# A routed attention and expert kernel: the bias of each exponential made on ScalarE instead of VectorE

## The chip, the cores and the metric

The kernel runs on one core of a Trainium2 chip. The metric is device time in microseconds (us) of one execution, as the median of several runs. A core has TensorE (PE in the rows, matrix products), VectorE (DVE), ScalarE (ACT), GpSimd (POOL) and SyncE (SP, which issues DMAs here). Each engine works through its own instructions in program order and waits on semaphores for the others.

## What is computed

Four batches of 12,288 queries attend to 768 pooled keys each (the keys are also the values), and every resulting row goes through one of eight experts, chosen by the largest of eight logits.

```python
kv_pool = kv.reshape(B, H // r, r, W // r, r, C).mean(axis=(2, 4))
k = v = kv_pool.reshape(B, -1, C) @ w_sr
s = scale * (q @ k.transpose(0, 2, 1))
s = s - s.max(-1, keepdims=True)
a = np.exp(s)
a /= a.sum(-1, keepdims=True) + 1e-09
x = (a @ v).reshape(B * S, D)
# per expert e, for the rows whose largest logit of x @ w_gate is e:
out[mask] = gate_w[mask, None] * eom[mask, e, None] * (np.maximum(x[mask] @ w1[e], 0.0) @ w2[e])
```

The part in question is `exp(s - s.max())`: for each row of scores the largest one is found, and the exponential is taken of the scaled scores less the scaled maximum.

## The kernel before

The 49,152 tokens are worked on in 96 groups of 512; a group is four blocks of 128 tokens, and four groups make a chunk, which is the unit of the routing (`routing`, 25 of them, since the last chunk is cut in two). The program's order is written out by hand: `for i in range(NG + OL)` goes over the groups, and eight steps `s` within each group emit the instructions of several groups at different stages. No scheduler moves anything afterwards.

In a step, in the order of the letters of `ORD` ("shxryfue"):

- **s**, `qk`, on even steps: TensorE makes the scores `S` of one block (128 tokens by 768 keys, in two PSUM banks, six products, L533 to L537; `S` has two buffers). VectorE takes the negated maximum of each row from PSUM into `nm[:, 0:1]` (L539) and, in an operation on one element per partition (L540), multiplies it by the row's factor `es` (a column of the tile `qm`) and adds the constant `PSH * log 2`: this is the bias, `nm[:, 1:2]`.
- **h**, `moe_h`: TensorE makes one of eight 128-row parts of the hidden layer, `H` (L864 to L866), ScalarE writes its rectified high half `HH` (L869) and VectorE the low half `HL` (L870). When `HL` is done the PSUM buffer of `H` is free. There are three such buffers (`psH`), shared with `U`, the sum over the values, and with the logits.
- **x**, `qk_exp`: ScalarE takes the exponential of the block, with `nm[:, 1:2]` as bias and `es` as scale, and sums the rows (L554). It waits for VectorE (the bias) and for GpSimd (the buffer of `pr`). In every second block `scale()` follows: VectorE's L899, which waits for the exponential.
- **r**, `qk_round`, a step later: ScalarE rounds `pr` to 16 bit (L567), GpSimd makes the remainder.
- **u** and **y**: TensorE's products with the values (L591, into `U`), and the second expert product (L879 to L881, into `Y`), which uses `HH` and `HL` of an earlier step.

`routing` adds some twenty small VectorE operations per chunk between these (L665 to L769), a piece a step. `es` and `nm` are columns of 128 partitions, read as one value per partition.

Of the kernel before, what the change touches and what calls it, by code (L numbers as in the profile page):

```python
# [20 lines left out]
F32 = mybir.dt.float32  # L21
# [4 lines left out]
AF = mybir.ActivationFunctionType  # L26
ALU = mybir.AluOpType
# [5 lines left out]
P = 128  # L33
# [13 lines left out]
PSH = 11  # L47
EPS = 1e-9
BIG = float(1 << 22)
LAG = 2  # L50
# [51 lines left out]
def body(ctx, tc, q, kv, w_sr, w_gate, w_og, w1, w2, out, cfg=Cfg):  # L102
    nc = tc.nc
    pe, act, dve, pool, sp = nc.tensor, nc.scalar, nc.vector, nc.gpsimd, nc.sync
# [22 lines left out]
    cst = ctx.enter_context(tc.tile_pool(name="cst", bufs=1))  # L127
# [45 lines left out]
    for n in sorted(set(n for _, n in UN)):  # L173
        runs[n] = cst.tile([P, E * n * GB], F32, name=f"run{n}")
        dve.memset(runs[n], 1.0)
        dve.memset(runs[n].rearrange("p (e b) -> p e b", e=E)[:, :, 0:1], 0.0)
    c13 = cst.tile([P, CG], F32, name="c13")
    dve.memset(c13, 2.0 ** -13)

# [334 lines left out]
    def qk(i, j):  # L514

        K2 = KVT[i // GPB][0]
        KH, KL = K2[:, 0, :], K2[:, 1, :]
        c, g = divmod(i, CG)
        es = QM[c][:, 2, g:g + 1]
        if j == 0:  # L520
            PTt[i] = wk.tile([P, 2 * NKB, GT], F16, tag="PT", bufs=2, name=f"PT{i}")
            if unit[i][1] == 0:
                SUMS[unit[i][0]] = rt.tile([P, CB], F32, tag="SUM", bufs=4, name=f"SUM{i}")
        S = psA.tile([P, 2, 512], F32, tag="A", name=f"S{i}_{j}")
        hk = [x for x in hooks if x[0] <= now[0]]
        if hk and (j in cfg.HJ or i <= OL):
            hooks.remove(hk[0])
            hk[0][1](S)
        m = i - OL - 1
        scale = moe_turn(m, j - 2, S) if j >= 2 and m >= 0 else None  # L530
        qh, ql = QS[i][:, j, :], QS[i][:, GB + j, :]
        for h in range(2):
            pe.matmul(S[:, h, 0:384], qh, KH[:, ts(h, 384)], start=True, stop=False)  # L533
        for h in range(2):
            pe.matmul(S[:, h, 0:384], qh, KL[:, ts(h, 384)], start=False, stop=False)  # L535
        for h in range(2):
            pe.matmul(S[:, h, 0:384], ql, KH[:, ts(h, 384)], start=False, stop=True)  # L537
        nm = wk.tile([P, 2], F32, tag="nm", bufs=4, name=f"nm{i}_{j}")
        dve.tensor_reduce(out=nm[:, 0:1], in_=S[:, :, 0:384], op=ALU.max, axis=AX.XY, negate=True)  # L539
        dve.tensor_scalar(nm[:, 1:2], nm[:, 0:1], es, PSH * math.log(2.0), op0=ALU.mult, op1=ALU.add)  # L540
        QX[(i, j)] = (S, nm, es, scale)
        if scale and j == GB - 1:
            OST.pop(m)
# [4 lines left out]
    def qk_exp(i, j):  # L548

        S, nm, es, scale = QX.pop((i, j))  # L550
        c, g = unit[i]
        pr = wk.tile([P, NK], F32, tag="pr", bufs=cfg.PRB, name=f"pr{i}_{j}")
        bl = g * GB + j
        act.activation(pr.rearrange("p (a k) -> p a k", a=2), S[:, :, 0:384], AF.Exp,  # L554
                       bias=nm[:, 1:2], scale=es, accum_out=SUMS[c][:, bl:bl + 1])
        PR[(i, j)] = pr
        if scale:
            scale()
# [329 lines left out]
    def moe_turn(i, h, S):  # L888

        ys = OST[i]  # L890
        c, g = unit[i]
        if h == 0:
            OT[i] = wk.tile([P, GB, C], F32, tag="o", name=f"o{i}")
        o = OT[i]
        for j in range(2):
            pe.transpose(S[:, j, 384:512], ys[:, ts(2 * h + j, P)], ident)

        def scale():
            dve.tensor_tensor(o[:, ts(h, 2), :], S[:, :, 384:512],  # L899
                              MSC[c][:, g * GB + 2 * h:g * GB + 2 * h + 2].unsqueeze(2).to_broadcast([P, 2, C]),  # L900
                              op=ALU.mult)
        return scale
# [159 lines left out]
    with tc.manual_schedule(engines={pool.engine, sp.engine, pe.engine, act.engine, dve.engine}):  # L1062
# [82 lines left out]
        for i in range(NG + OL):  # L1145
# [5 lines left out]
            for s in range(8):  # L1151
# [11 lines left out]
                for o in cfg.ORD if mi >= 0 else cfg.ORDA:  # L1163
# [4 lines left out]
                    if o == "s" and att and s % 2 == 0:  # L1168
                        qk(i, s // 2)
                        while late:  # L1170
                            qk_round(*late.pop(0))
                    if o == "x" and att and s % 2 == 0:
                        qk_exp(i, s // 2)
# [86 lines left out]
        while events:  # L1260
            i, s = divmod(min(events), 8)
# [7 lines left out]
def kernel_body(tc, q, kv, w_sr, w_gate, w_og, w1, w2, out, cfg=Cfg):  # L1269
    with ExitStack() as ctx:  # L1270
        body(ctx, tc, q, kv, w_sr, w_gate, w_og, w1, w2,
             out.rearrange("(b n) c -> b n c", b=cfg.NB), cfg)
# [28 lines left out]
```

## Time and profile before

| | us |
|---|---|
| median of three runs (lowest, highest) | 1921.08 (1918.65, 1921.35) |
| the profiled execution, its own time | 1917.69 |
| its span, first to last instruction | 1916.0 |
| TensorE busy in it | 1862.5 (97%) |
| VectorE busy | 1460.6 (76%) |
| ScalarE busy | 1317.8 (69%) |
| GpSimd busy | 1251.3 (65%) |

The granted clock of TensorE is 0.995 of full speed over the span. A busy TensorE is modelled from overlapping products, so what counts for it is the time in which it stood still and who ended that.

### The profile page before, as it was taken

Reading aid. Unit: us, or ns where it says so; the run is one execution under the profiler, and the core shown is the slowest. Engines: PE = TensorE matmul, PEld = TensorE weight load, DVE = VectorE, ACT = ScalarE, POOL = GpSimd, SP = SyncE. Lnnn points to the kernel's source line nnn. Section 1 sums busy time; section 2 is a strip of 40 time slices with the busy share of each in tenths; the row PEclk is TensorE's granted clock in tenths of the full one; section 3 lists DMA queues with packets and bytes.
Section 4 is the critical chain, followed back from the end, with each engine's and each line's share of the span. In section 5 each row is a group of like instructions: output and inputs, shape, how many; then the busy total and the mean of one; then the engine's idle time right before and its main releaser. Section 6 shows DMA issues by size and latency. Waiting matters only on the chain. (4 is left out here: it accounts for less than half of the span.)

```text
span 1916.0 us, 31565 instructions
## 1 busy us (share of the span) xinstructions
PE 1862.5 (97%) x10225; PEld 951.3 (50%) x10225; DVE 1460.6 (76%) x2984; ACT 1317.8 (69%) x2391; POOL 1251.3 (65%) x1426
## 2 busy tenths in 40 slices
PE   6899999999999999999999999999999999999978
PEld 5444455554545555545545555544455455554534
DVE  6776877778878778778787777787787877776754
ACT  3777767677776776676777767766777767676733
POOL 2548677676586777774767867856657557567561
PEclk9999999999999999999999999999999999999999
DMA  8888889888888988887979888877978788877632
GB/s 236 161 161 164 179 167 174 166 161 179 178 164 179 176 159 180 167 165 154 194 149 189 176 178 176 174 152 149 187 146 167 152 160 154 156 153 147 133 73 71
DMA packets 884021, 311.67 MB, mean 163 GB/s; under 512 B 827584, under 2 KB 833857, under 8 KB 883856
## 3 DMA queue, kind: packets, MB, share of 16 engines
q1 hardware_dynamic: 870944, 309.18, 79.8%
q0 software_dynamic: 12480, 0.40, 0.6%
q8 instruction: 81, 1.33, 0.3%
q14 instruction: 84, 0.69, 0.1%
q10 hardware_dynamic: 432, 0.07, 0.0%
HBM read 56.83 MB, written 51.25 MB: 56 GB/s over the span
## 5 line engine op out<-in xcount | busy, mean ns | idle before, releaser
L120 POOL TENSOR_TENSOR ph<-pr,ph 128x384 f16<-128x384 f32 (+1 forms) x760 | 711.6, 936 | 493.1 <-issue 417.5
L870 DVE SCALAR_TENSOR_TENSOR HL<-H,HH 128x512 f16<-128x512 f32 x768 | 526.9, 687 | 166.3 <-ACT HH L869 135.1
L869 ACT ACTIVATE HH<-H 128x512 f16<-128x512 f32 x768 | 456.0, 594 | 234.6 <-PE H L866 197.9
L554 ACT ACTIVATE pr<-S,nm,qm 128x768 f32<-128x768 f32 x384 | 380.6, 991 | 249.3 <-DVE nm L540 219.1
L779 POOL DMA_INDIRECT scr<-rw,idx x384 | 386.2, 1006 | 98.2 <-issue 81.2
L539 DVE TENSOR_REDUCE nm<-S 128x1 f32<-128x768 f32 x384 | 363.2, 946 | 74.3 <-PE S L537 50.1
L591 PE MATMUL U<-PT,V 128*128 128x512 f16 (+1 forms) x1746 | 406.2, 378 | 8.3 <-DVE HL L870 5.1
L567 ACT ACTIVATE ph<-pr 128x768 f16<-128x768 f32 x380 | 320.3, 843 | 2.5 <-DMA PT<-ph 2.0
L864 PE MATMUL H<-U,w 128*128 128x512 f16 x768 | 291.5, 380 | 7.8 <-DVE HL L870 4.4
L879 PE MATMUL Y<-HH,w 128*128 128x512 f16 x768 | 291.3, 379 | 1.8 <-ACT HH L869 1.0
L881 PE MATMUL Y<-HL,w 128*128 128x512 f16 x768 | 291.0, 379 | 0.9 <-DVE HL L870 0.6
L866 PE MATMUL H<-U,w 128*128 128x512 f16 x768 | 291.5, 380 | 0.0
L865 PE MATMUL H<-U,w 128*128 128x512 f16 x768 | 291.5, 380 | 0.0
L880 PE MATMUL Y<-HH,w 128*128 128x512 f16 x768 | 291.1, 379 | 0.0
L591 PEld LDWEIGHTS <-V 128*128 128x128 f16 x1746 | 171.3, 98 | 214.6 <-issue 10.9
L533 PE MATMUL S<-K,qT 128*128 128x384 f16 x768 | 188.1, 326 | 5.8 <-ACT pr L554 3.5
L537 PE MATMUL S<-K,qT 128*128 128x384 f16 x768 | 188.0, 327 | 1.3 <-DVE qT L504 1.0
L535 PE MATMUL S<-K,qT 128*128 128x384 f16 x768 | 188.0, 326 | 0.5 <-DVE K L394 0.5
L899 DVE TENSOR_TENSOR o<-S,msw 128x256 f32<-128x256 f32 x176 | 74.7, 425 | 98.3 <-ACT pr L554 91.3
L120 POOL TENSOR_TENSOR kvs<-kvs 128x256 f32<-128x256 f32 (+2 forms) x148 | 108.1, 731 | 20.9 <-DMA kvs<-in_kv_dram 9.9
L880 PEld LDWEIGHTS <-w 128*128 128x128 f16 x768 | 75.2, 98 | 91.0 <-issue 3.7
L866 PEld LDWEIGHTS <-w 128*128 128x128 f16 x768 | 75.2, 98 | 91.0 <-issue 0.6
(209 smaller groups left out, 1815.4 us busy)
## 6 DMA issues: line engine op xcount, KB each, us to landing
kvs<-in_kv_dram SPq DMA_DIRECT2D x96, 256.0 KB
q<-in_q_dram SPq DMA_DIRECT2D x96, 256.0 KB
urows<-uT SPq DMA_DIRECT2D x96, 256.0 KB
out_dram<-o SPq DMA_DIRECT2D x96, 256.0 KB
PT<-ph SPq DMA_TRANSPOSE x384
scr<-rw,idx POOLq DMA_INDIRECT x384
wr<-in_moe_w_dram SPq DMA_DIRECT2D x8, 512.0 KB
tw<-in_moe_w_dram SPq DMA_DIRECT2D x4, 512.0 KB
```

Of the source, the lines that this page charges most:

```text
L120: ins = pool.tensor_tensor(*a, **k)
L539: dve.tensor_reduce(out=nm[:, 0:1], in_=S[:, :, 0:384], op=ALU.max, axis=AX.XY, negate=True)
L554: act.activation(pr.rearrange("p (a k) -> p a k", a=2), S[:, :, 0:384], AF.Exp, bias=nm[:, 1:2], scale=es, accum_out=SUMS[c][:, bl:bl + 1])
L567: act.activation(ph[:, 0, :], pr, AF.Copy)
L591: pe.matmul(PVP[i][:, cols], ops[n][0], ops[n][1][:, cols], start=(n == 0), stop=(n == len(ops) - 1))
L779: ins = pool.indirect_dma_start(out=scr, out_offset=bass.IndirectOffsetOnAxis(ap=idx[:, bl:bl + 1], axis=0), in_=rw[:, bl, :], in_offset=None,
L864: pe.matmul(H, w1h[:, ts(f, P)], UH, start=True, stop=False)
L865: pe.matmul(H, w1h[:, ts(f, P)], UL, start=False, stop=False)
L866: pe.matmul(H, w1l[:, ts(f, P)], UH, start=False, stop=True)
L869: act.activation(HH, H, AF.Relu)
L870: dve.scalar_tensor_tensor(HL, H, 0.0, HH, op0=ALU.max, op1=ALU.subtract)
L880: pe.matmul(Y, w2l[:, ts(f, P)], HH, start=False, stop=False)
```

## The change

From the fourth group on (`i > LAG`, 93 of 96 groups, 372 of 384 blocks) VectorE no longer makes the bias. ScalarE makes it in front of each exponential, with an `Identity` activation on one element per partition that reads the maximum, a column `shift` holding the constant, and `es`.

```diff
+    shift = cst.tile([P, 1], F32, name="shift")
+    dve.memset(shift, PSH * math.log(2.0))
...
         dve.tensor_reduce(out=nm[:, 0:1], in_=S[:, :, 0:384], op=ALU.max, axis=AX.XY, negate=True)
-        dve.tensor_scalar(nm[:, 1:2], nm[:, 0:1], es, PSH * math.log(2.0), op0=ALU.mult, op1=ALU.add)
+        if i <= LAG:
+            dve.tensor_scalar(nm[:, 1:2], nm[:, 0:1], es, PSH * math.log(2.0), op0=ALU.mult, op1=ALU.add)
...
         bl = g * GB + j
+        if i > LAG:
+            act.activation(nm[:, 1:2], nm[:, 0:1], AF.Identity, bias=shift, scale=es)
         act.activation(pr.rearrange("p (a k) -> p a k", a=2), S[:, :, 0:384], AF.Exp,
                        bias=nm[:, 1:2], scale=es, accum_out=SUMS[c][:, bl:bl + 1])
```

On ScalarE, the first two blocks of group 66 stand like this before (`pr` is the exponential, `ph` its rounding, `HH` the hidden layer's high half, `z` a step of the routing; the numbers behind names are buffers):

```order
L869 ACTIVATE HH_7_16038<-H_7_16034 128x512
L554 ACTIVATE pr_0_16042,SUM_15527<-S_0_16024,nm_0_16031,qm_14338 128x768
L869 ACTIVATE HH_0_16062<-H_0_16058 128x512
L567 ACTIVATE ph_0_16066<-pr_0_16042 128x768
L735 ACTIVATE z_16021<-z_16021 128x16
L869 ACTIVATE HH_1_16091<-H_1_16087 128x512
L554 ACTIVATE pr_1_16095,SUM_15527<-S_1_16075,nm_1_16084,qm_14338 128x768
L884 ACTIVATE ys_16105<-Y_15917 128x512
```

and like this in the changed program:

```order
L874 ACTIVATE HH_7_16039<-H_7_16035 128x512
L558 ACTIVATE nm_0_16033<-nm_0_16033,shift,qm_14340 128x1
L559 ACTIVATE pr_0_16043,SUM_15529<-S_0_16026,nm_0_16033,qm_14340 128x768
L874 ACTIVATE HH_0_16064<-H_0_16060 128x512
L572 ACTIVATE ph_0_16068<-pr_0_16043 128x768
L740 ACTIVATE z_16023<-z_16023 128x16
L874 ACTIVATE HH_1_16092<-H_1_16088 128x512
L558 ACTIVATE nm_1_16086<-nm_1_16086,shift,qm_14340 128x1
L559 ACTIVATE pr_1_16096,SUM_15529<-S_1_16077,nm_1_16086,qm_14340 128x768
L889 ACTIVATE ys_16107<-Y_15919 128x512
```

One operation (L558) stands in front of each exponential (now L559); it waits for VectorE's maximum, and the exponential now waits for ScalarE's own L558 and for GpSimd. Nothing else moved on this engine, and the program holds one load of activation tables as before.

On VectorE, the same two blocks before (`nm` the maximum and the bias, `HL` the hidden layer's low half, `st` a step of the routing):

```order
L539 TENSOR_REDUCE nm_0_16031<-S_0_16024 128x1
L540 TENSOR_SCALAR nm_0_16031<-nm_0_16031,qm_14338 128x1
L870 SCALAR_TENSOR_TENSOR HL_7_16039<-H_7_16034,HH_7_16038 128x512
L460 TENSOR_REDUCE qm_15309<-q_15778 128x1
L466 SCALAR_TENSOR_TENSOR qm_15309<-qm_15309,c_123 128x4
L467 RECIPROCAL qm_15309<-qm_15309 128x4
L733 TENSOR_TENSOR z_16021<-z_16021,rinv_15890 128x16
L870 SCALAR_TENSOR_TENSOR HL_0_16063<-H_0_16058,HH_0_16062 128x512
L539 TENSOR_REDUCE nm_1_16084<-S_1_16075 128x1
L540 TENSOR_SCALAR nm_1_16084<-nm_1_16084,qm_14338 128x1
L870 SCALAR_TENSOR_TENSOR HL_1_16092<-H_1_16087,HH_1_16091 128x512
L711 SCALAR_TENSOR_TENSOR st_15999<-S_1_16075,ebase 128x8
```

and in the changed program:

```order
L541 TENSOR_REDUCE nm_0_16033<-S_0_16026 128x1
L875 SCALAR_TENSOR_TENSOR HL_7_16040<-H_7_16035,HH_7_16039 128x512
L462 TENSOR_REDUCE qm_15311<-q_15780 128x1
L468 SCALAR_TENSOR_TENSOR qm_15311<-qm_15311,c_125 128x4
L469 RECIPROCAL qm_15311<-qm_15311 128x4
L738 TENSOR_TENSOR z_16023<-z_16023,rinv_15892 128x16
L875 SCALAR_TENSOR_TENSOR HL_0_16065<-H_0_16060,HH_0_16064 128x512
L541 TENSOR_REDUCE nm_1_16086<-S_1_16077 128x1
L875 SCALAR_TENSOR_TENSOR HL_1_16093<-H_1_16088,HH_1_16092 128x512
L716 SCALAR_TENSOR_TENSOR st_16001<-S_1_16077,ebase 128x8
```

The one-element operation behind each maximum is gone, and `HL` follows the maximum directly. TensorE, GpSimd and the DMA queues have the same instructions in the same order.

## Rows read from the trace of the kernel before

**Rows 1.** The page: span, and TensorE's busy time

```profile
span 1916.0 us, 31565 instructions
...
PE 1862.5 (97%) x10225; PEld 951.3 (50%) x10225; DVE 1460.6 (76%) x2984; ACT 1317.8 (69%) x2391; POOL 1251.3 (65%) x1426
```

**Rows 2.** Busy time by stretch: the long middle, and one stretch of 80 us

```profile
80.00:1760.00 1680.00, 1666.79 (x9146) 843.42 (x9144) 1312.24 (x2608) 1201.13 (x2175) 1147.43 (x1307) 1.00 0.84 166
...
1440.00:1520.00 80.00, 80.00 (x439) 40.36 (x438) 61.32 (x122) 58.48 (x104) 52.06 (x58) 1.00 0.80 160
```

**Rows 3.** Waits: who for whom, us in total, times, longest

```profile
PE U L591 <- DVE HL L870: 5.1, 7, 1.8
PE H L864 <- DVE HL L870: 4.4, 8, 1.1
...
PE H L864 <- DVE U L596: 2.8, 5, 1.0
...
DVE o L899 <- ACT pr L554: 91.3, 163, 1.6
```

**Rows 4.** Timeline of TensorE, two stalls: start, us, what, idle time before it

```profile
1269.69 0.38 PE L864 MATMUL H<-U,w 128*128 128x512 f16 x1 [0.64 <-DVE HL L870]
...
1270.76 0.38 PE L879 MATMUL Y<-HH,w 128*128 128x512 f16 x1 [0.26 <-ACT ys L884]
```

**Rows 5.** Timeline of VectorE ahead of these two stalls

```profile
1261.15 0.42 DVE L899 TENSOR_TENSOR o<-S,msw 128x256 f32<-128x256 f32 x1 [0.61 <-ACT pr L554]
...
1264.34 0.95 DVE L539 TENSOR_REDUCE nm<-S 128x1 f32<-128x768 f32 x1
1265.33 0.21 DVE L540 TENSOR_SCALAR nm<-nm,qm 128x1 f32<-128x1 f32 x1
1265.46 0.68 DVE L870 SCALAR_TENSOR_TENSOR HL<-H,HH 128x512 f16<-128x512 f32 x1
...
1267.24 0.69 DVE L870 SCALAR_TENSOR_TENSOR HL<-H,HH 128x512 f16<-128x512 f32 x1
1267.85 0.95 DVE L539 TENSOR_REDUCE nm<-S 128x1 f32<-128x768 f32 x1
1268.83 0.21 DVE L540 TENSOR_SCALAR nm<-nm,qm 128x1 f32<-128x1 f32 x1
1268.96 0.68 DVE L870 SCALAR_TENSOR_TENSOR HL<-H,HH 128x512 f16<-128x512 f32 x1
1270.25 0.17 DVE L711 SCALAR_TENSOR_TENSOR st<-S,ebase 128x8 f32<-128x8 f32 x1 [0.61 <-ACT pr L554]
```

**Rows 6.** Timeline of ScalarE ahead of the same two stalls

```profile
1260.04 0.99 ACT L554 ACTIVATE pr<-S,nm,qm 128x768 f32<-128x768 f32 x1 [1.51 <-DVE nm L540]
...
1265.64 0.99 ACT L554 ACTIVATE pr<-S,nm,qm 128x768 f32<-128x768 f32 x1 [2.32 <-DVE nm L540]
...
1266.62 0.59 ACT L869 ACTIVATE HH<-H 128x512 f16<-128x512 f32 x1
...
1269.14 0.99 ACT L554 ACTIVATE pr<-S,nm,qm 128x768 f32<-128x768 f32 x1 [0.61 <-DVE nm L540]
1270.03 0.19 ACT L554 ACTIVATION_READ_ACCUMULATOR pr<-S,nm,qm 128x1 f32 x1
1270.12 0.58 ACT L884 ACTIVATE ys<-Y 128x512 f32<-128x512 f32 x1
```

**Rows 7.** Groups of ScalarE: busy us, mean ns of one, idle before, who ended it

```profile
L554 ACT ACTIVATE pr<-S,nm,qm 128x768 f32<-128x768 f32 x384 | 380.6, 991 | 249.3 <-DVE nm L540 219.1 <-POOL ph L120 8.4 <-DVE nm L539 7.7
L567 ACT ACTIVATE ph<-pr 128x768 f16<-128x768 f32 x380 | 320.3, 843 | 2.5 <-DMA PT<-ph 2.0
...
L481 ACT ACTIVATE q<-q,qm 128x512 f16<-128x512 f32 x93 | 66.8, 718 | 0.1
...
L614 ACT ACTIVATE lgp<-lg,g 128x512 f32<-128x512 f32 (+2 forms) x25 | 16.7, 669 | 15.3 <-PE H L866 10.4 <-PE S L537 3.7 <-PE lg L609 1.3
...
L735 ACT ACTIVATE z<-z 128x16 f32<-128x16 f32 (+2 forms) x25 | 5.3, 212 | 0.1
```

## The prediction

> **What bounds the kernel now.** I begin with the page and the stretches. TensorE is busy for 1862.5 of 1916.0 us [rows 1]. Between 80 and 1760 us, away from start and end, it stands still for only 1680.00 - 1666.79 = 13.2 us [rows 2]; of the 21 stretches of 80 us in there, seven show it busy for 80.00, as the one that stands in the rows, and 14 less. So the kernel is bound by TensorE's own work, and a change on two other engines can move the time only through those stalls: nothing to win beyond some 13 us, and something to lose wherever a stall becomes longer.
>
> Next, the waits. TensorE's stalls are mostly waits for a buffer of `H`, `U` and the logits, which VectorE frees: 5.1 + 4.4 us on `HL`, 2.8 us on the low half of `U`, 20 waits of 0.6 us on average [rows 3]. Then the timelines of one of them, the stall at 1269.69 us [rows 4], read backwards. `HL` at 1268.96 frees the buffer; before it VectorE went without a pause from `HL` at 1267.24 through the maximum at 1267.85 and L540 [rows 5]. `HL` at 1267.24 began 0.03 us after `HH` ended (1266.62 + 0.59), and that `HH` stood behind the exponential of 1265.64, which had waited 2.32 us for L540 [rows 6]. The maximum ahead of it, at 1264.34, came at the end of a run of routing steps that began behind L899 at 1261.15, and L899 had waited for the exponential of 1260.04, again one that waited for L540 [rows 5, 6]. So where TensorE stalls, two engines take turns in one chain: maximum, bias, exponential, then `HH` and `HL` or L899, next maximum. From the maximum of 1264.34 to that of 1267.85 this loop takes 3.51 us, with no slack in it. The second stall, at 1270.76, hangs on the exponential of 1269.14 through `ys` at 1270.12 [rows 4, 6].
>
> **The change, part by part.** What VectorE loses: 372 operations of 0.21 us [rows 5]. In time this is more, since L540 waits for the maximum and `HL` could not overlap with it. The maximum ended at 1265.29 and `HL` began at 1265.46, 0.17 later; between `HL` and the maximum of 1267.85, where no wait stands, the second begins 0.08 us before the first ends (1267.24 + 0.69 = 1267.93) [rows 5]. So `HL` behind a maximum comes up to 0.25 us earlier, where its `HH` is there.
>
> What ScalarE gains: 372 operations on one element with two operands read per partition, of a kind that the trace doesn't have. The slope per element is (843 - 212) / (768 - 16) = 0.84 ns, so the fixed part without such an operand is 212 - 13 = 199 ns. With one of them (L481: 718 - 430) it is 288, so one costs about 90; two give some 380 ns for the new operation. The exponential itself, with two, has 991 - 645 = 346 from PSUM, which agrees [rows 7]. Bounds: 0.20 us if such operands cost nothing here, 0.39 at the most. I take 0.38, because L481 and L554 both show the operands' cost.
>
> The Trainium skill (VectorE: DVE Perf Modes, "The TRN2 errata") gives a ScalarE operation from SBUF to SBUF a fixed 224 cycles whatever its operands, an estimate of 0.19 us here; by it the sum would be the third rival's below. The trace's L481 has 288 ns where that rule has 187, so here the measurement decides against it.
>
> The chain gets longer. Before, the exponential began 0.35 us behind the maximum's end (1265.29 to 1265.64) [rows 5, 6]. After, two hand-overs remain, maximum to L558 and L558 to the exponential. A hand-over costs between 0.03 (`HH` to `HL` above) and 0.10 us (L540's end at 1265.54 to 1265.64); I take one of each, the long one in front of the exponential, which keeps two waits. So 0.03 + 0.38 + 0.10 = 0.51: each exponential that waits for its bias starts **0.16 us later**. Bounds: 0.06 + 0.20 - 0.35 = -0.09, and 0.20 + 0.39 - 0.35 = +0.24. Where `HH` ends just as the bias would have come, L558 can't begin before it, and the price is about 0.38 + 0.10 - 0.10 = 0.38 or a little less. Queued behind the exponential on ScalarE are `HH`, L567, and the high halves of `U` and `q`; VectorE's L899 waits for it 163 times [rows 3], and through these TensorE.
>
> ScalarE as a whole has room: 1317.8 + 372 x 0.38 = 1459 us of 1916, and it now idles 249.3 us in front of the exponentials alone [rows 1, 7]. VectorE falls to about 1381. Neither total matters to TensorE. Outside of the routing's chains the 0.16 us is hidden: three `H` buffers and two of `S` lie between, and TensorE runs without a pause in a third of the stretches [rows 2].
>
> **The sum.** It goes by the routing chains, of which there are 25 (L614 once each) [rows 7]. In the chain shown, the first stall has the exponentials of 1260.04 and 1265.64 behind it and ends in an `HL` right behind a maximum: 2 x 0.16 - 0.25 = +0.07 us. The second has three and no such `HL`: 3 x 0.16 = +0.48, and that is what TensorE loses at this place in all. Chains go on before the rows shown, as long as each link finds the other engine waiting, and others end early or with the relief; I take 0.4 us per chain. Two thirds of the stretches have stalls now: 25 x 2/3 x 0.4 = 6.7 us. In the other third the slack takes about half: 25 x 1/3 x 0.2 = 1.7. The cases at the higher price, ScalarE's stretches with weights to split, and the last blocks, behind which nothing covers, add some 1.6 by choice. Together **+10 us**. Against its own time the profiled execution would be 1917.69 + 10 = 1928; that execution lies 3.4 us below the median 1921.08 and just under the lowest run, so against the median it is 1931. I give 1930.
>
> About 0.2%, 3.8 us, is what a measurement of this kernel tells from no change.
>
> **The rivals.**
> - *Absorbed.* The chains end at TensorE only where the slack is gone, and the earlier `HL` pays for part: if three stalls in four end as the first one did (+0.07) and the rest by +0.48, the 25 chains cost 25 x 0.17 = 4, with the slack of a third of them 3 us. For it: 0.25 us of relief per block on the engine that frees the buffers. Against: L899 and the routing steps behind it come after the exponential, so the relief is waited away there. Time 1923 and less, around 1922.
> - *ScalarE falls behind.* If most exponentials pay the higher price of 0.38, three links cost 1.1 us, and the 25 chains 20 to 28 us with little slack left. For it: `HH` is in the loop too. Against: idle time in front of the exponentials is 249.3 / 384 = 0.65 us on average [rows 7], so `HH` is usually long done. It decides where this idle time is mostly under 0.1 us. Time around 1943.
> - *Faster.* The operand reads cost nothing on so small an operation: L558 takes 0.20, a hand-over 0.03 and 0.10, and the exponential begins 0.33 us behind the maximum, 0.02 earlier than before. Then only the relief is left: the 15 waits on `HL` [rows 3] become up to 0.25 shorter, 3.8 us, and chains of three links gain 25 x 0.06 = 1.5. It decides from an operation of about 0.22 us down. Time 1916. Against: L481 and L554 pay for their operands every time [rows 7].
> - *The change doesn't do what it says* can't be: the order shows the operation gone from one engine and present on the other.
>
> **How the numbers follow.** Forecast, slower by 4 to 17 us, 0.55; absorbed 0.24; ScalarE behind 0.13; faster 0.08. That gives slower 0.68, same 0.24, faster 0.08. The time is the forecast's. The range leaves out the faster case and a little of the absorbed one below, and the upper part of the second rival: 1919 to 1943.
>
> **What would show it.** L558 at about 380 ns; from the maximum's end to the exponential's start 0.51 us instead of 0.35; the maximum followed by `HL` with no gap; the wait of L899 for the exponential up from 91.3 us, by 0.16 and 0.25 more a time, to around 140 to 160; TensorE's idle time from 80 to 1760 us up from 13.2 to about 22, on the same lines and at the routing of each chunk. Wrong if L558 takes 0.2 us, if TensorE's stalls stay at 13 us though the exponentials start later, or if idle time in front of ScalarE's exponentials vanishes and `HH` is late everywhere.

## The result and the profile after

The changed kernel takes 1943.51 us (median, 1942.52 to 1944.83) against 1921.21 of the kernel before, 22.3 us more: a ratio of 1.0118, 95% interval 1.0106 to 1.0130. The forecast was 1930, some 9 us more than before, with a range up to 1943. Slower was right; the loss was more than twice the one given, and the time lies just above the range.

The page of the changed kernel, its span and the busy times, answers to [rows 1]:

```profile
span 1940.8 us, 31851 instructions
...
PE 1867.7 (96%) x10225; PEld 948.9 (49%) x10225; DVE 1383.1 (71%) x2613; ACT 1437.6 (74%) x2763; POOL 1248.8 (64%) x1426
```

VectorE gave up 77.5 us, as costed. ScalarE took on 119.8 where 141 were costed: the new operations take 143.3 by themselves (L558 below), and some overlap with the instruction ahead. Neither engine is near its limit. The same long middle as in [rows 2]:

```profile
80.00:1760.00 1680.00, 1650.65 (x9027) 830.90 (x9025) 1222.28 (x2226) 1295.97 (x2495) 1123.87 (x1285) 1.00 0.83 164
```

TensorE now stands still for 29.4 us of it instead of 13.2, at the full granted clock, and gets through 9027 products instead of 9146. (Over the whole span its idle time grew by 19.6 of the 24.8 us between the two profiled executions. The other 5.2 stand as busy time, in which the ends of products are modelled; what they are is not shown.)

The waits, which answer to [rows 3]; the first line is of the kernel before, the others of the changed one:

```profile
DVE HL L870 <- ACT HH L869: 135.1, 174, 2.5
...
DVE HL L875 <- ACT HH L874: 231.9, 311, 3.2
...
DVE o L904 <- ACT pr L559: 147.4, 158, 2.2
...
PE H L869 <- DVE HL L875: 8.6, 16, 1.1
PE U L596 <- DVE HL L875: 7.7, 15, 0.8
...
PE H L869 <- DVE U L601: 4.3, 5, 1.4
```

TensorE waits on the same producers as before, only oftener: on `HL` 31 times instead of 15, 16.3 us instead of 9.5. VectorE waits longer for ScalarE: `HL` for `HH` 231.9 us, which was 135.1, and L904 (L899 before) 147.4, which was 91.3.

The groups of ScalarE, which answer to [rows 7], and the timeline of the exponential of one block, VectorE's part of it first:

```profile
L559 ACT ACTIVATE pr<-S,nm,qm 128x768 f32<-128x768 f32 x384 | 380.7, 991 | 50.8 <-DVE nm L543 8.9 <-POOL ph L120 7.3 <-PE S L539 0.5
...
L558 ACT ACTIVATE nm<-nm,shift,qm 128x1 f32<-128x1 f32 x372 | 143.3, 385 | 194.8 <-DVE nm L541 189.5 <-DVE wmb L822 2.8 <-issue 1.8
```

```profile
743.83 0.95 DVE L541 TENSOR_REDUCE nm<-S 128x1 f32<-128x768 f32 x1
744.70 0.68 DVE L875 SCALAR_TENSOR_TENSOR HL<-H,HH 128x512 f16<-128x512 f32 x1
...
744.82 0.39 ACT L558 ACTIVATE nm<-nm,shift,qm 128x1 f32<-128x1 f32 x1 [2.01 <-DVE nm L541]
745.30 0.99 ACT L559 ACTIVATE pr<-S,nm,qm 128x768 f32<-128x768 f32 x1
```

The new operation takes 385 ns. The maximum ends at 744.78, L558 begins 0.04 later and the exponential 0.09 behind its end: 0.52 us in all, 0.17 more than before. `HL` begins 0.08 us before the maximum's end.

### The profile page after: what moved, and what is told of

It reads as the page before. It is cut to its first block, busy times and chain, and to the rows that moved or that the text cites. A ratio compares the mean times of both kernels' runs of the same rounds, so it can differ in the third digit from the quotient of the medians.

```text
span 1940.8 us, 31851 instructions
## 1 busy us (share of the span) xinstructions
PE 1867.7 (96%) x10225; PEld 948.9 (49%) x10225; DVE 1383.1 (71%) x2613; ACT 1437.6 (74%) x2763; POOL 1248.8 (64%) x1426
## 5 line engine op out<-in xcount | busy, mean ns | idle before, releaser
L875 DVE SCALAR_TENSOR_TENSOR HL<-H,HH 128x512 f16<-128x512 f32 x768 | 526.7, 686 | 263.3 <-ACT HH L874 231.9
L559 ACT ACTIVATE pr<-S,nm,qm 128x768 f32<-128x768 f32 x384 | 380.7, 991 | 50.8 <-DVE nm L543 8.9
L558 ACT ACTIVATE nm<-nm,shift,qm 128x1 f32<-128x1 f32 x372 | 143.3, 385 | 194.8 <-DVE nm L541 189.5
L904 DVE TENSOR_TENSOR o<-S,msw 128x256 f32<-128x256 f32 x176 | 74.8, 425 | 161.4 <-ACT pr L559 147.4
L885 PEld LDWEIGHTS <-w 128*128 128x128 f16 x768 | 75.1, 98 | 95.0 <-issue 8.9
```

The lines of the kernel that those rows point to most:

```text
L875: dve.scalar_tensor_tensor(HL, H, 0.0, HH, op0=ALU.max, op1=ALU.subtract)
L885: pe.matmul(Y, w2l[:, ts(f, P)], HH, start=False, stop=False)
```

## The experiments

Theory A: the price is the longer way from maximum to exponential, and it counts where the routing makes the engines take turns. Theory B: the price is ScalarE's time for 372 more operations. On the chips of the experiments the kernel before takes 1897 to 1898 us, so each is compared with the runs of before beside it. Below, the *way* of a block is the time from the end of its maximum to the start of its exponential.

**Where the operations stand.** The change in a part of the groups only, in four kernels with one condition each:

```diff
-        if i > LAG:
+        if i > LAG and i % CG in (1, 2):      # e1: groups 1 and 2 of each chunk, with the routing's steps
+        if i > LAG and i % CG not in (1, 2):  # e2: groups 0 and 3
+        if i > LAG and i % CG == 1:           # e9: group 1 alone
+        if i > LAG and i % CG == 2:           # e10: group 2 alone
             act.activation(nm[:, 1:2], nm[:, 0:1], AF.Identity, bias=shift, scale=es)
```

(VectorE makes the bias in the other groups.) Expected of groups 1 and 2: 

> The change only in the groups 1 and 2 of each chunk (i % 4 in 1, 2), where the routing's VectorE steps stand; half of the operations are moved. Theory A (the price is the longer way from maximum to exponential, 0.17 us per link, and it counts where routing chains maximum, exponential and VectorE together): most of the loss is here, +14 to +20 us against before. Theory B (the price is ScalarE's time for 372 more operations, wherever they stand): half of the loss, about +11 us.

Expected of groups 0 and 3: 

> The change only in the groups 0 and 3 of each chunk. Theory A: little, -2 to +6 us against before, the +6 where the chain runs on into group 3. Theory B: half of the loss, about +11 us.

Measured: groups 1 and 2 cost 19.0 us (1916.70 against 1897.72, ratio 1.0097, 1.0081 to 1.0112), groups 0 and 3 cost 2.7 us (1.0015, 1.0006 to 1.0024). About the same number of operations (184 and 188) and seven times the price, as theory A said; theory B is out as the main cause.

Expected of group 1: 

> The change only in group 1 of each chunk, where the routing chain begins (a quarter of the operations). If every link of a chain adds its delay and the sum counts where TensorE stalls (theory A with six or so links a chain), groups 1 and 2 share the 19 us of both: 5 to 12 us slower than before. Rival (only the two or three links right before a stall count, most of them in group 2): 0 to 4 us slower.

Expected of group 2: 

> The change only in group 2 of each chunk, where the chain ends. With links that add up: 7 to 14 us slower than before, and with the run for group 1 about 19 together. Rival: nearly all of it, 15 to 20 us slower.

Measured: 10.4 us (1907.81 against 1897.41, ratio 1.0053, 1.0039 to 1.0067) and 7.6 us (1.0037, 1.0023 to 1.0051), together 18.0 of the 19.0 of both. The links early in a chain, a group ahead of some stalls, cost no less than the late ones. The rival, that only the last two or three links count, falls.

**The same work out of the way.** VectorE makes the bias as before, ScalarE runs the operation for nothing (`spare1` is a tile that nobody reads):

```diff
-        if i <= LAG:
-            dve.tensor_scalar(nm[:, 1:2], nm[:, 0:1], es, PSH * math.log(2.0), op0=ALU.mult, op1=ALU.add)
+        dve.tensor_scalar(nm[:, 1:2], nm[:, 0:1], es, PSH * math.log(2.0), op0=ALU.mult, op1=ALU.add)
...
-            act.activation(nm[:, 1:2], nm[:, 0:1], AF.Identity, bias=shift, scale=es)
+            act.activation(spare1, nm[:, 0:1], AF.Identity, bias=shift, scale=es)
```

Expected: 

> VectorE makes the bias as before, and ScalarE runs the same Identity operation in front of each exponential into a tile that nobody reads. ScalarE's work is that of the changed kernel, but where ScalarE was idle the exponential need not start later than before. Theory A: 0 to +8 us against before (the rest from exponentials right behind HH, which the spare operation delays by up to 0.3 us). Theory B: the whole loss or more, since VectorE has no relief, +22 us and over.

Measured: 1.2 us more (1898.95 against 1897.72, ratio 1.0008, 0.9999 to 1.0017), which can't be told from nothing. Its timeline shows why:

```profile
735.14 0.95 DVE L541 TENSOR_REDUCE nm<-S 128x1 f32<-128x768 f32 x1
736.13 0.21 DVE L543 TENSOR_SCALAR nm<-nm,qm 128x1 f32<-128x1 f32 x1
...
736.13 0.39 ACT L559 ACTIVATE sp<-nm,shift,qm 128x1 f32<-128x1 f32 x1 [2.01 <-DVE nm L541]
736.44 0.99 ACT L560 ACTIVATE pr<-S,nm,qm 128x768 f32<-128x768 f32 x1
```

Here the spare operation runs in the time in which ScalarE waits for the bias anyway, and the exponential begins 0.35 us behind the maximum's end (736.09 to 736.44), as before. It isn't so everywhere: where `HH` ends late the spare operation does hold the exponential up, and over all 372 blocks of the trace the way is 0.05 us longer than before on average. 372 operations of 0.39 us are almost free when nothing depends on them.

**The way longer and shorter.** First the operation with one operand less:

```diff
-            act.activation(nm[:, 1:2], nm[:, 0:1], AF.Identity, bias=shift, scale=es)
+            act.activation(nm[:, 1:2], nm[:, 0:1], AF.Copy, bias=PSH * math.log(2.0), scale=es)
```

Expected: 

> The changed kernel with a Copy that has its constant as an immediate, so that only the scale is read per partition. The operation should take about 0.295 instead of 0.386 us, and an exponential start 0.08 instead of 0.17 us later than before. Theory A: the loss goes with this delay, half of it or a little less stays, +9 to +12 us. Theory B: it goes with the operation's length, three quarters stay, about +17 us.

Measured: 8.1 us more than before (1905.80 against 1897.72, ratio 1.0051, 1.0037 to 1.0064), a little under what A said and half of what B said; the ratio's interval, 7 to 12 us, takes in A's 9 to 12 and leaves out B's 17. VectorE's maximum and ScalarE's two operations:

```profile
738.85 0.95 DVE L541 TENSOR_REDUCE nm<-S 128x1 f32<-128x768 f32 x1
...
739.84 0.29 ACT L558 ACTIVATE nm<-nm,qm 128x1 f32<-128x1 f32 x1 [2.00 <-DVE nm L541]
740.22 0.99 ACT L559 ACTIVATE pr<-S,nm,qm 128x768 f32<-128x768 f32 x1
```

The exponential comes 0.42 us behind the maximum. Next, no new operation on ScalarE, but two steps on VectorE, from the fourth group on:

```diff
-        dve.tensor_scalar(nm[:, 1:2], nm[:, 0:1], es, PSH * math.log(2.0), op0=ALU.mult, op1=ALU.add)
+        dve.tensor_scalar(nm[:, 2:3], nm[:, 0:1], es, None, op0=ALU.mult)
+        dve.tensor_scalar(nm[:, 1:2], nm[:, 2:3], PSH * math.log(2.0), None, op0=ALU.add)
```

Expected: 

> VectorE makes the bias in two dependent operations (multiply, then add), ScalarE has nothing new. The exponential should start 0.25 us later than before. Theory A: 0.25 / 0.17 of the changed kernel's loss, 25 to 38 us slower than before, though ScalarE does no more than before. Rival (the loss has to do with ScalarE's new operation): 2 to 6 us slower, for 372 more short operations on VectorE.

Measured: 20.4 us more than before (1918.46 against 1898.11, ratio 1.0106, 1.0090 to 1.0121). ScalarE has not one operation more, and most of the loss is there. It is under the 25 to 38 expected:

```profile
746.01 0.95 DVE L539 TENSOR_REDUCE nm<-S 128x1 f32<-128x768 f32 x1
746.99 0.21 DVE L543 TENSOR_SCALAR nm<-nm,qm 128x1 f32<-128x1 f32 x1
747.24 0.15 DVE L544 TENSOR_SCALAR nm<-nm 128x1 f32<-128x1 f32 x1
...
747.49 0.99 ACT L558 ACTIVATE pr<-S,nm,qm 128x768 f32<-128x768 f32 x1 [2.50 <-DVE nm L544]
```

The second step takes 0.15 us, not 0.21, and the exponential is 0.53 behind the maximum, 0.19 later than before and not 0.25. By the rule of the expectation that would still be 25 to 28 us (0.19 / 0.17 of the changed kernel's loss): the rule took 0.17 for the changed kernel's delay, which is more in many blocks, as the table below shows. Then two kernels without any bias operation. In both the maximum is taken but not subtracted, so that part of the computation is left out; the exponential is tied by hand to an earlier VectorE instruction (from the fourth group on, shown in short):

```diff
+    x = act.activation(pr.rearrange("p (a k) -> p a k", a=2), S[:, :, 0:384], AF.Exp,
+                       bias=shift, scale=es, accum_out=SUMS[c][:, bl:bl + 1])
+    tc.add_manual_dep(x.ins, behind[0], ...)   # e5: the maximum; e7: the HL that follows it
```

Expected behind the maximum: 

> From the fourth group on no engine makes the bias: the exponential takes the constant column as its bias (the maximum is still taken and waited for, but not subtracted, so this part of the computation is left out). The exponential should start about 0.10 us behind the maximum instead of 0.35. Theory A (the time follows the way from maximum to exponential): 0.25 us less per link, 8 to 14 us faster than before, as much as the stalls that are left allow. Rival: before, the stalls came from VectorE's routing steps alone and not from this way, so a shorter way saves nothing that is measured, 0 to 3 us faster.

Expected behind `HL`: 

> As the kernel without any bias operation, but the exponential waits for the low half HL that follows the maximum on VectorE, so that it starts about 0.70 us behind the maximum, 0.36 later than before, while no engine does more and VectorE does less. Theory A: 30 to 55 us slower than before. Rival (work counts, not the way): no slower than before.

Measured: tied to the maximum 1886.10 against 1898.11, 12.0 us faster (ratio 0.9939, 0.9926 to 0.9953); tied to `HL` 1968.20, 70.1 us slower (1.0372, 1.0358 to 1.0386), more than the 55 expected at the most. The first, with the maximum's end and the exponential's start:

```profile
729.13 0.95 DVE L541 TENSOR_REDUCE nm<-S 128x1 f32<-128x768 f32 x1
...
730.17 0.99 ACT L559 ACTIVATE pr<-S,shift,qm 128x768 f32<-128x768 f32 x1 [1.91 <-DVE nm L541]
```

and the second:

```profile
761.56 0.95 DVE L541 TENSOR_REDUCE nm<-S 128x1 f32<-128x768 f32 x1
762.42 0.68 DVE L879 SCALAR_TENSOR_TENSOR HL<-H,HH 128x512 f16<-128x512 f32 x1
...
763.20 0.99 ACT L559 ACTIVATE pr<-S,shift,qm 128x768 f32<-128x768 f32 x1 [2.67 <-DVE HL L879]
```

0.09 and 0.69 us behind the maximum. The two have the same instructions and differ in the one wait; 82 us lie between them. Behind `HL` the exponential also waits for what `HL` waits for, `HH` and TensorE, so its way is over 1 us in a good third of the blocks; the expectation counted 0.36 us a link.

**A shorter way with all of the work.** The exponential's second wait is for the buffer of `pr`. With four buffers it falls away: the trace has 8 semaphore instructions in front of the exponentials instead of 384. (The reason, as argued from the program: an earlier wait of ScalarE, for a transfer that came after GpSimd's work, covers it.)

```diff
-    PRB = 2
+    PRB = 4
```

Expected of the kernel before with this: 

> The kernel before with four buffers for pr instead of two. The exponential then has one wait, for the bias, and none for GpSimd, and should start 0.035 us behind it instead of 0.095. Theory A: 0.06 us less per link, 2 to 6 us faster than before. Rival (so small a step is lost in slack, or the exponentials' hand-over doesn't depend on the number of waits): within 0.1 per cent of before.

Measured: 1893.79 against 1897.41, 3.6 us faster (ratio 0.9979, 0.9970 to 0.9988). Its timeline:

```profile
735.05 0.95 DVE L539 TENSOR_REDUCE nm<-S 128x1 f32<-128x768 f32 x1
736.04 0.21 DVE L540 TENSOR_SCALAR nm<-nm,qm 128x1 f32<-128x1 f32 x1
...
736.29 0.99 ACT L554 ACTIVATE pr<-S,nm,qm 128x768 f32<-128x768 f32 x1 [2.26 <-DVE nm L540]
```

The exponential begins 0.04 us behind the bias instead of 0.10. Ten real waits for GpSimd's buffer, 8.4 us in [rows 7], are gone too, and no run separates the two savings. This version computes all that the reference does and beats both kernels.

All of these side by side, in us: the way of the block shown (for the kernel before from [rows 5, 6]), its mean over the 372 blocks from the fourth group on in each trace, and the time against before:

| kernel | way, block shown | mean way | time |
|---|---|---|---|
| no bias operation | 0.09 | 0.16 | -12.0 |
| before, four buffers | 0.29 | 0.30 | -3.6 |
| before | 0.35 | 0.38 | 0 |
| spare operation | 0.35 | 0.43 | +1.2 |
| one operand | 0.42 | 0.52 | +8.1 |
| two steps on VectorE | 0.53 | 0.56 | +20.4 |
| the change, run again | 0.52 | 0.61 | +25.0 |
| behind `HL` | 0.69 | 0.88 | +70.1 |

The time follows the mean way, whichever engine lengthens it, though not in proportion. The block shown has nearly the shortest way of its kernel. In the changed kernel 142 of the 372 blocks have one over 0.06 us longer than that, in the kernel before 23 and with two steps on VectorE 20: these are mostly blocks where `HH` ends behind the maximum, and L558 has to wait for it where VectorE's bias did not. So the changed kernel has the shorter way in the block shown and the longer one on average, and is the dearer of the two.

**One chain, link by link.** For this the changed kernel and the kernel before were run again. Expected: 

> The changed kernel once more, on the chip of these runs: 1.0 to 1.3 per cent slower than before, as the first time.

> The kernel before unchanged, for a profile on the chip of these runs: equal to before, with the exponentials 0.345 us behind the maximum's end and the same places of TensorE's stalls.

Measured: the change costs 25.0 us there (1923.07 against 1898.11, ratio 1.0137, 1.0121 to 1.0152), a little over the 1.3 per cent expected; the kernel before took 1897.83 in one run. Below, group 1 and three blocks of group 2 of one chunk: first the last scores of blocks 0, 3, 6 and 7 on TensorE and the seven exponentials of blocks 0 to 6, before:

```profile
711.32 0.49 PE L537 MATMUL S<-K,qT 128*128 128x384 f16 x2
...
725.61 0.49 PE L537 MATMUL S<-K,qT 128*128 128x384 f16 x2
...
738.74 0.49 PE L537 MATMUL S<-K,qT 128*128 128x384 f16 x2
...
744.93 0.49 PE L537 MATMUL S<-K,qT 128*128 128x384 f16 x2
```

```profile
713.15 0.99 ACT L554 ACTIVATE pr<-S,nm,qm 128x768 f32<-128x768 f32 x1
...
718.03 1.00 ACT L554 ACTIVATE pr<-S,nm,qm 128x768 f32<-128x768 f32 x1
...
723.19 0.99 ACT L554 ACTIVATE pr<-S,nm,qm 128x768 f32<-128x768 f32 x1 [1.27 <-DVE nm L540]
...
729.87 0.99 ACT L554 ACTIVATE pr<-S,nm,qm 128x768 f32<-128x768 f32 x1 [2.33 <-DVE nm L540]
...
735.45 0.99 ACT L554 ACTIVATE pr<-S,nm,qm 128x768 f32<-128x768 f32 x1 [2.31 <-DVE nm L540]
...
739.21 0.99 ACT L554 ACTIVATE pr<-S,nm,qm 128x768 f32<-128x768 f32 x1 [0.61 <-DVE nm L540]
...
743.39 0.99 ACT L554 ACTIVATE pr<-S,nm,qm 128x768 f32<-128x768 f32 x1 [0.29 <-DVE nm L540]
```

And the same blocks in the changed kernel, with two stalls of TensorE behind block 6's scores:

```profile
722.72 0.49 PE L539 MATMUL S<-K,qT 128*128 128x384 f16 x2
...
737.32 0.49 PE L539 MATMUL S<-K,qT 128*128 128x384 f16 x2
...
750.44 0.49 PE L539 MATMUL S<-K,qT 128*128 128x384 f16 x2
...
752.10 0.38 PE L869 MATMUL H<-U,w 128*128 128x512 f16 x1 [0.52 <-DVE HL L875]
...
753.58 0.38 PE L884 MATMUL Y<-HH,w 128*128 128x512 f16 x1 [0.68 <-ACT ys L889]
...
757.68 0.49 PE L539 MATMUL S<-K,qT 128*128 128x384 f16 x2
```

```profile
723.89 0.60 ACT L874 ACTIVATE HH<-H 128x512 f16<-128x512 f32 x1 [1.05 <-PE H L871]
724.39 0.38 ACT L558 ACTIVATE nm<-nm,shift,qm 128x1 f32<-128x1 f32 x1
724.86 0.99 ACT L559 ACTIVATE pr<-S,nm,qm 128x768 f32<-128x768 f32 x1
...
729.74 0.99 ACT L559 ACTIVATE pr<-S,nm,qm 128x768 f32<-128x768 f32 x1
...
735.10 0.99 ACT L559 ACTIVATE pr<-S,nm,qm 128x768 f32<-128x768 f32 x1
...
742.27 0.99 ACT L559 ACTIVATE pr<-S,nm,qm 128x768 f32<-128x768 f32 x1
...
748.03 0.99 ACT L559 ACTIVATE pr<-S,nm,qm 128x768 f32<-128x768 f32 x1
...
751.96 0.99 ACT L559 ACTIVATE pr<-S,nm,qm 128x768 f32<-128x768 f32 x1
...
756.30 0.99 ACT L559 ACTIVATE pr<-S,nm,qm 128x768 f32<-128x768 f32 x1
```

TensorE's scores are 11.40 us later than before at block 0, 11.71 at block 3 and 11.70 at block 6. The exponentials are 11.71 later at blocks 0 and 1, then 11.91, 12.40, 12.58, 12.75 and 12.91.

At blocks 0 and 1 the delay against TensorE's 11.40 is 0.31 us, since L558 stands right behind `HH` (at block 0 it begins at 724.39, over the last 0.10 us of `HH`). It isn't carried from block 0 to block 1, where ScalarE waits for TensorE's `H` again; the chain begins at block 1. From block 2 to 3 it grows by 0.49, and 0.32 of this is not the way: two routing steps on VectorE (L687 and L697) took 2.08 us together, and 1.76 before (as L682 and L692), for a reason that isn't shown. From block 3 to block 6 TensorE loses nothing and each exponential falls 0.16 to 0.18 us further behind: every one is a link. At block 6 the sum is 12.91 - 11.70 = 1.21 us. Behind it TensorE stalls by 0.52 and 0.68 us, where the kernel before has only the second stall, with 0.26, and the scores of block 7 are 757.68 - 744.93 = 12.75 us later. So TensorE lost 12.75 - 11.40 = 1.35 us over this chain.

The other chains are alike on average. Taken by the starts of the maxima in the two traces, over the 23 chunks from the second on, the changed kernel falls 1.3 us further behind from the first block of group 1 to the last of group 2 (0.8 of it in group 1), and 0.2 come back by the next group 1. With the change in group 1 alone it is 0.8 us, all in group 1; in group 2 alone 0.6, all but nothing of it in group 1. The links add up.

## Why the prediction was right or wrong

- **What bounds the kernel, and how the chain runs**: right. The loss is in the groups with the routing (19.0 of the 21.7 us that the two halves have together), and TensorE stalls on `HL`, `ys` and `U` as before.
- **The price of one exponential**: right for the plain one. 0.38 us was taken for L558 and 0.16 for the delay; measured are 385 ns and 0.17. That the operands cost nothing, as the third rival had it, is refuted by the one-operand kernel: 0.29 us for its operation against 0.39 in the timelines above. The higher price, for exponentials behind `HH`, was taken as rare and put, with other things, at "some 1.6 by choice"; about a third of the blocks pay it in part (0.31 in blocks 0 and 1 above), and the mean delay is 0.23. So this term was mis-sized too.
- **The relief of VectorE**: its size was right (`HL` begins 0.08 us before the maximum's end instead of 0.17 behind it), its worth was not borne out. I let chains end with 0.25 us given back; but `HL` now waits for `HH` 231.9 instead of 135.1 us, since `HH` stands behind the later exponential. What the relief is worth by itself no run separates.
- **L899's wait**: 140 to 160 us forecast, 147.4 measured.
- **The sum**: here the prediction failed, in "I take 0.4 us per chain". The two chains read for it showed two and three exponentials, the text said that they go on before the rows shown, and the value was not raised for it. (Nor were its two stalls all that TensorE lost there: the trace has a third in the same chain, 0.45 us at 1260.60 behind `HL`.) In the chain followed above the delay has grown to 1.21 us at its sixth link and TensorE loses 1.35; all 25 chains lose 25.0 us, 1.0 each, in that comparison and 0.9 each in the first. With 1.21 in place of 0.4 the prediction's own sum comes to about 25 x (2/3 x 1.2 + 1/3 x 0.6) + 1.6 = 27 us, with the 25.0 measured. One chain stands for all in this, so it checks the size and no more. Idle time of TensorE from 80 to 1760 us, 22 us forecast, came to 29.4 for the same reason.
- **The second rival**, ScalarE falling behind, named the time (1943) and not the cause. Its own sign, idle time vanishing in front of the exponentials, did not come: 194.8 + 50.8 us of idle time stand in front of L558 and the exponential, where 249.3 were, and the spare operation costs 1.2 us. What it said of exponentials behind `HH` holds for a third of them, not for most. That this makes the change 4.6 us dearer than the two steps on VectorE fits the mean delays (0.23 against 0.19 us, a ratio near that of 25.0 to 20.4); no run separates it. That its time was met is luck: it counted three links at 0.38 us, and the chains have six or seven at about 0.2.
- **Absorbed, and faster**: neither. Slack in front of TensorE hides a chain only in part, and the operands cost what L481 and L554 show.

## What to carry to other kernels

Where two engines take turns in a chain that the bounding engine waits for, an operation costs the delay from input to output times the links of the chain, less what slack takes back, and not its busy time: 372 spare operations cost about 1 us, the same ones in the way 25. Before such a sum is made, follow a chain back to the link that waited for the bounding engine and count all of its links; the last three are not the chain. Then look at the delay in all blocks, not in one: the block first read had the plain 0.17 us, the mean was 0.23. And in such a chain look at the hand-overs too: four buffers in place of two, and with them one wait less in front of the exponential, were worth 3.6 us.

## What the runs showed of the hardware that was not expected

A ScalarE instruction with two waits began 0.10 us behind the one it waited for, with one wait 0.04 (the kernel with four buffers against before). A ScalarE operation that needed the result of the one ahead began 0.09 us behind its end (L558 at 744.82, the exponential at 745.30), while one that didn't began 0.10 us before it (`HH` and L558 at block 0). Operands read per partition cost about 0.09 us each even on one element: 0.39 us with two, 0.29 with one, 0.21 with none and 16 elements (L735 in [rows 7]); the functions differ too. On VectorE an operation on one element took 0.21 us with such an operand and 0.15 without. And the same program, the kernel before, took 1921 us in the first comparison and 1897 to 1898 on the chips of the experiments; what makes this difference is not shown. Of the 19.9 us between the two profiled executions only 4.1 have come up by the last maximum, so it lies mostly behind the chains.
